# Splits for the second MoE tied to the first MoE's last block, and eight of its w_in blocks made float32 earlier

## The chip, the cores and the metric

The kernel runs on one core of a Trainium2 chip. The time is device microseconds (us) of one execution; "PE" is TensorE, "DVE" VectorE, "ACT" ScalarE, "POOL" GpSimd, "SP" the engine whose queue issues the DMAs.

## The reference

Causal attention with decay, then two mixture-of-experts layers (here plain two-layer blocks, called MoE 1 and MoE 2) over the same 2304 tokens. All inputs are float64 or float32 as NumPy draws them; the four weights are float64 here.

```python
attn = softmax(scale * q @ k.T + decay)       # 4 batches, 8 heads, 576 tokens, head size 64
x = (attn @ v) as 2304 x 512
h = x @ moe_w_in                               # 512 x 2048
x = (h * clip(h + 3, 0, 6) / 6) @ moe_w_out    # 2048 x 512
h = x @ moe2_w_in
out = softplus(h) @ moe2_w_out
```

## The kernel before

**Number format.** TensorE multiplies in a short format (fp32r), so every float32 operand is split into a high part (a copy by ACT in the short format) and a low part (original less high, by DVE or POOL), and each product is three matmuls.

**The order of the work.** Nothing is issued in the order of the program text. Every operation is registered with `op` or `dma` (lines 118 and 352) with the engines that may run it, an estimated cost, the keys that it reads (`r`) and writes (`w`), and a due time `at`. A planner, `Work.order` (line 152), then simulates the engines: at each step it takes the operation that can start first on its engine, and among those that can start equally early the one with the smallest `at`. Its result is the program order of each engine, fixed before the kernel runs. Engines work through their queues in order; a key read that another engine writes becomes a semaphore wait.

**MoE 1** works on five blocks of tokens: blocks 0 to 3 have 512, block 4 (`LAST_B`) 256. The 2048 inner columns are 16 units `ft` of 128. A unit of a block is 12 matmuls of the first product (`g1`, line 1299) into one PSUM bank, ACT's relu (line 1339), DVE's product (line 1341, its last reader of the bank, so the bank is free after it), the split of the result (copy, line 1319 or 1320; rest on DVE, line 1322), and 12 matmuls of the second product (`moe1_g2`, line 1362) that accumulate into four bank areas. The accumulators are evicted after unit 15 (lines 1390 and 1391); those of blocks 0 to 2 go through the two staging tiles `st`. Blocks 0, 1 and 2 run while attention of the next batch is computed in between. Blocks 3 and 4 run interleaved, unit by unit, and alone: their accumulators hold six of the eight banks, which leaves banks 2 and 3 for the first products. Relus of block 4 are the 256-wide ones in the trace.

**MoE 2** uses Strassen-like forms with seven products. Stage A (line 1415) works on 576 tokens by one pair `p` of units at a time, eight pairs; stage B (line 1516) follows. Before stage A can run, during blocks 3 and 4, these are prepared:

- `weights2_in(0, p, ...)`: the w_in of pair p, two blocks of 512 KB in float64. `raw_weights` (line 989) loads one and makes it float32 by bit operations: one on ACT (line 1017) and three on DVE (lines 1019, 1020, 1023). For p = 0, 2, 4, 6, 7 the tiles `st` stage it, for p = 1, 3, 5 the tile `HY`. Then four sums (line 1107) and three splits (lines 1136 on ACT, 1139 on DVE or POOL) make its seven operands in `rW`.
- `weights2_out(p, ...)`, p = 0 to 6: the w_out of pair p, float32 already in `wf_dram`; four sums (line 1107), seven splits (1136, 1139) into a ring in `XO`, seven stores to `wo_dram` (line 1166).
- `factors_x(0, ...)`: the first 576 tokens; four sums (line 1221) and seven splits (lines 1215, 1216).

**Conversions ahead of time.** `early2` (line 1068) loads one float64 block of MoE 2's weights to `st[0]` or `st[1]` in turn, makes it float32 and stores it to `wf_dram` (line 1073). The dictionary `early` (line 1566) says at which unit of which block: w_out blocks 0 to 7 at the even units of block 1, 8 to 15 at those of block 2. All others are in `late2` and are converted by `weights2`. Since `early2` of unit (t, 0) is registered ahead of the evictions of block t - 1 and uses the same `st`, these evictions come after it.

Of the kernel before, what the change touches and what calls it, by code (L numbers as in the profile page):

```python
# [273 lines left out]
def attention_two_moe_kernel(  # L274
# [22 lines left out]
    NF = moe_w_out.shape[0] // P  # L297
    TB = 512
    NB = (NT + TB - 1) // TB
    LAST_B = NB - 1  # L300
# [29 lines left out]
    op = wk.op  # L330
# [63 lines left out]
    three = mp.tile([P, 1], F32, name="three")  # L394
# [644 lines left out]
    def either(n, fn, late=K["pv"]):  # L1039

        return [("dve", dve(n), lambda: fn(nc.vector), late), ("pool", 2.8 * n + 60, lambda: fn(nc.gpsimd))]
# [30 lines left out]
        raw_weights(i, 1, o, ft, at, True)  # L1072
        dma(lambda: nc.sync.dma_start(out=wf_dram[o, ft], in_=words(i)[:, 0]), 4 * P * NC * P, r=[("stage", i), ("up", i)], w=[("wf", o, ft)], at=at - K["cvw"], name="storewf")

    def weights2(o, p, at, parts, i0):

        own = i0 >= 8

        def raw(i):
            return BIG["XO"][:, (i - 8) * NC * P:(i - 7) * NC * P].bitcast(F32)  # L1080

        for z in range(2):
            i, ft = i0 + z, 2 * p + z
            if not own and (o, ft) in late2:
                raw_weights(i, 1, o, ft, at, True)
                continue

            def load(i=i, ft=ft):
                dst = raw(i) if own else words(i)[:, 0]
                if wide:  # L1090
                    nc.sync.dma_start(out=dst, in_=wf_dram[o, ft])
                else:
                    nc.sync.dma_start(out=dst.rearrange("p (c f) -> p c f", c=NC) if o == 0 else dst, in_=w_source(1, o, ft))

            dma(load, 4 * P * NC * P, w=[("stage", i), ("up", i)] + [("o", i, 0), ("o", i, 1)] * (i < 2), r=["m2"] * (i in (2, 3) or own) + [("wf", o, ft)],
                at=at - 15, name="loadwf")
        h = 2 * P

        def x(i, e, j, n=1):
            if own:  # L1100
                return (BIG["XT"][:, i * 2 * h:] if e else raw(i0 + i))[:, j * h:(j + n) * h]
            return words(i0 + i)[:, e, j * h:(j + n) * h]


        def sums(dst, a, b, sub, r, w, name):
            def go(e):
                e.tensor_tensor(x(*dst), x(*a), x(*b), op=ALU.subtract if sub else ALU.add)
            op(either(h, go), r=r, w=w, at=at - 2, name=name)

        s0, s1, u0, u1 = ((x, 8 + i if own and x == "up" else i0 + i) for x in ("stage", "up") for i in range(2))  # L1110
        X11, X12, X21, X22 = (0, 0, 0), (0, 0, 1), (1, 0, 0), (1, 0, 1)
        Ca, Cb, Cc, Cd = (0, 1, 0), (0, 1, 1), (1, 1, 0), (1, 1, 1)
        if o == 0:
            sums(Ca, X21, X22, False, [s0, s1], [u0], "S1")
            sums(Cb, Ca, X11, True, [s0], [u0], "S2")
            sums(Cc, X11, X21, True, [s0, s1], [u1], "S3")
            sums(Cd, X12, Cb, True, [s0, u0], [u1], "S4")
        else:
            sums(Ca, X12, X11, True, [s0, s1], [u0], "T1")
            sums(Cb, X22, Ca, True, [s1], [u0], "T2")  # L1120
            sums(Cc, X22, X12, True, [s0, s1], [u1], "T3")
            sums(Cd, X21, Cb, True, [s1, u0], [u1], "T4")
        place = dict(zip(AT[o], ((0, 0, 0), (0, 0, 1), (0, 1, 0), (0, 1, 1), (1, 1, 0), (1, 1, 1), (1, 0, 1)) if o == 0 else
                         ((1, 0, 0), (1, 0, 1), (1, 1, 0), (1, 1, 1), (0, 1, 0), (0, 1, 1), (0, 0, 0))))
        for z0, z1, dst, w, then in parts:
            i, e, j = place[AT[o][z0]]
            n = z1 - z0

            def src(i=i, e=e, j=j, n=n):
                return words(i0 + i) if n == 4 else x(i, e, j, n)  # L1130

            def to(s, dst=dst, n=n):
                return dst(s).rearrange("p (e n) -> p e n", e=2) if n == 4 else dst(s)

            rd = [(s0, s1)[i], (u0, u1)[i]]
            op(("act", act(n * h, False), lambda src=src, to=to: nc.scalar.activation(out=to(0), in_=src(), func=ACTF.Copy)), r=rd, w=w, at=at, name="w2h")

            def lo(e, src=src, to=to):
                e.tensor_tensor(to(1), src(), to(0).bitcast(F32), op=ALU.subtract)  # L1139

            op(either(n * h, lo), r=rd, w=w, at=at, name="w2l")
            then()
# [15 lines left out]
    def weights2_out(p, at, i0):  # L1158

        parts = []  # L1160
        for z in range(7):
            i = pieces[0] % NPC
            pieces[0] += 1

            def store(z=z, i=i):
                dma(lambda: nc.sync.dma_start(out=wo_dram[p].rearrange("p (s z f) -> p s z f", s=2, z=7)[:, :, z], in_=piece(i).bitcast(F32)), 16 * P * P,
                    r=[("piece", i)], w=[("wo", p, z)], at=at, name="storewo")

            parts.append((z, z + 1, lambda s, i=i: piece(i)[:, s], [("piece", i)], store))
        weights2(1, p, at, parts, i0)  # L1170

    def load_wo(p, at):
        dma(lambda: nc.sync.dma_start(out=unit2_w(p).rearrange("p s z f -> p (s z f)").bitcast(F32), in_=wo_dram[p]), 4 * P * UW,
# [13 lines left out]
    def factors_x(t, at, step):  # L1187

        z = t % 2

        def pace(x):
            return [("pace", t - 1, x)] if t else []

        def sm(i):
            return BIG["XT"][:, i * n:(i + 1) * n].rearrange("p (c n) -> p c n", c=2)

        n = 2 * HA
        for f, c0, h in (("B11", 0, 0), ("B21", 2, 0), ("B22", 2, 1), ("B12", 0, 1)):
            a, done = t * NA + h * HA, 0
            while done < HA:  # L1200
                t1, o = divmod(a + done, TB)
                m = min(HA - done, tokens(t1) - o)

                def go(f=f, c0=c0, t1=t1, o=o, m=m, done=done):
                    to = sm(0) if f == "B12" else xf(z, f, 1).bitcast(F32)
                    nc.sync.dma_start(out=to[:, :, done:done + m], in_=x2_dram[t1][c0:c0 + 2, :, o:o + m].rearrange("c p s -> p c s"))

                dma(go, 8 * P * m, r=[("x2", t1, c) for c in (c0, c0 + 1)] + ["m2"], w=[("xt", 0) if f == "B12" else ("xf", z, f)], at=at, name="loadx2")
                done += m

        def raw(f):
            return xf(z, f, 1).bitcast(F32)

        def split(f, src, key, at, x):
            op(("act", act(n, False), lambda: nc.scalar.activation(out=xf(z, f, 0), in_=src(), func=ACTF.Copy)), r=[key] + pace(x), w=[("xf", z, f)], at=at, name="xfh")
            op(either(n, lambda e: e.tensor_tensor(xf(z, f, 1), src(), xf(z, f, 0).bitcast(F32), op=ALU.subtract)), r=[key], w=[("xf", z, f)], at=at, name="xfl")


        for i, (f, d, a, b) in enumerate((("T3", 1, "B22", 0), ("T1", 0, 0, "B11"), ("T2", 1, "B22", 0), ("T4", 1, "B21", 1))):
            def go(e, d=d, a=a, b=b):  # L1220
                e.tensor_tensor(sm(d), *((sm(y) if isinstance(y, int) else raw(y)) for y in (a, b)), op=ALU.subtract)  # L1221

            key = [("xt", y) if isinstance(y, int) else ("xf", z, y) for y in (a, b)]
            op(either(n, go), r=key + ["m2"] + pace(i), w=[("xt", d)], at=at + step * i, name="x" + f)
            split(f, lambda d=d: sm(d), ("xt", d), at + step * (i + 0.5), i)
        for i, f in enumerate(("B11", "B21", "B22")):
            split(f, lambda f=f: raw(f), "m2", at + step * (4 + i), 4 + i)
# [104 lines left out]
    def moe1_g1(t, ft):  # L1332
        at = moe_at(t, ft)
        n = tokens(t)
        bk = g1(0, t, ft, at, sorted({b for b, _ in acc_of(t)}) if ft == 0 else ())
        i, i3 = next_unit(t >= LAST_B - 1)
        g = gt[i][:, 0:n]
        ev = at - K["evb"]
        op(("act", act(n, True, 1), lambda: nc.scalar.activation(out=g, in_=bank[bk.i][:, 0:n], func=ACTF.Relu, bias=three)),  # L1339
           r=["three"], banks=[bk], w=[("g", i)], at=ev, name="relu")  # L1340
        op(("dve", dve(n), lambda: nc.vector.scalar_tensor_tensor(  # L1341
            out=g, in0=g, scalar=6.0, in1=bank[bk.i][:, 0:n], op0=ALU.min, op1=ALU.mult)),
           banks=[bk], w=[("g", i)], at=ev, name="g")
        split_g(g, i, i3, n, ev + K["splag"], 2)
        G[0, t, ft] = i3
# [217 lines left out]
        for o in range(2):  # L1563
            weights(o, ft, moe_at(0, ft) - K["cv"] + o * 2)

    early = {(1 + n // 8, n % 8 * 2): (1, n) for n in range(NF)} if wide else {}
    late2 = [(o, ft) for o in range(2) for ft in range(NF) if wide and (o, ft) not in early.values()]
    units = [(t, ft) for t in range(NB - 2) for ft in range(NF)]
    units += [(t, ft) for ft in range(NF) for t in (NB - 2, NB - 1)]
    for n in range(len(units) + 1):  # L1570
        if n < len(units):
            t, ft = units[n]
            if (t, ft) == (NB - 2, 0):
# [3 lines left out]
                at = moe_at(t, 0) - K["xl"]  # L1577
# [6 lines left out]
            if ft == NF - 1 and t + 1 < NB - 1:  # L1584

                at = moe_at(t + 1, 0) - K["xl"]
# [85 lines left out]
```

## Time and profile before

| | |
|---|---|
| timed runs | 1029.60, 1035.90, 1037.64 us; median 1035.9 |
| profiled execution | 1029.02 us |
| its span, first to last instruction | 1026.8 us |
| busy in the span | PE 95%, DVE 82%, ACT 58%, POOL 25% |

The 2.2 us between span and time lie outside the program. Times in the rows are us from the start of the span. Roughly: attention with blocks 0, 1 and 2 runs to 490, blocks 3 and 4 to 648, stage A to 836, stage B to the end. A line such as "PE ... [3.65 <-DVE GT L1341]" says that the engine sat idle for 3.65 us before it and what it waited for last.

### The profile page before, as it was taken

To read this page: it belongs to the slowest core of one execution; us is meant where nothing else is said; L and a number is where in the kernel's file an instruction comes from. 1 tells how busy PE (TensorE), PEld (TensorE's weight loads), DVE (VectorE), ACT (ScalarE), POOL (GpSimd) and SP (SyncE) were. 2 spreads that over 40 slices of the span, in tenths; PEclk is the share of its full clock that TensorE was granted. 3 is DMA by queue.
4 is the path that set the end of the run, shared out by engine and by line. 5 is a ranking of instruction groups with operands and counts; after the bars stand their busy time and mean duration, and the time that the engine had idled before them with its cause. 6 is when DMAs were issued, how large, how long until landed. Compare 5 with 4: busy or idle time off the path is not lost. (4 is left out here: it accounts for less than half of the span.)

```text
span 1026.8 us, 17687 instructions
## 1 busy us (share of the span) xinstructions
PE 979.6 (95%) x6116; PEld 849.7 (83%) x6116; DVE 843.0 (82%) x1671; ACT 596.5 (58%) x1300; POOL 255.7 (25%) x246
## 2 busy tenths in 40 slices
PE   8999998989999999999898899999999999999997
PEld 6666677768788888888787788899999999999997
DVE  8789879999998669986889886787787758888885
ACT  6899666778666556664454443665555544443342
POOL 2221332230000000000447532220010307454542
PEclk9999999999999999999999999999999999999999
DMA  6675553445553235412768550444333994445342
GB/s 139 165 156 144 132 154 100 110 143 148 141 146 93 61 115 144 117 47 68 238 210 264 165 173 11 162 145 146 131 122 143 346 368 138 124 135 152 108 126 77
DMA packets 189682, 149.12 MB, mean 145 GB/s; under 512 B 107948, under 2 KB 163660, under 8 KB 188696
## 3 DMA queue, kind: packets, MB, share of 16 engines
q1 hardware_dynamic: 189592, 147.99, 48.4%
q8 instruction: 48, 0.79, 0.3%
q14 instruction: 42, 0.34, 0.1%
HBM read 97.58 MB, written 50.37 MB: 144 GB/s over the span
## 5 line engine op out<-in xcount | busy, mean ns | idle before, releaser
L1299 PE MATMUL bank<-MX,W 128*128 128x512 f32 x768 | 224.5, 406 | 6.3 <-DVE GT L1341 5.6
L1362 PE MATMUL bank<-MX,W 128*128 128x512 f32 (+1 forms) x688 | 188.8, 383 | 3.6 <-DVE MX L1322 3.6
L1299 PEld LDWEIGHTS bank<-MX,W 128*128 128x128 f32 x768 | 133.9, 191 | 28.9 <-DVE GT L1341 6.1
L1362 PEld LDWEIGHTS bank<-MX,W 128*128 128x128 f32 x688 | 121.3, 189 | 25.9 <-DVE MX L1322 4.8
L1516 PE MATMUL bank<-rW,rW 128*128 128x256 f32 x1134 | 138.6, 283 | 1.9 <-POOL rW L1139 0.9
L1516 PEld LDWEIGHTS bank<-rW,rW 128*128 128x128 f32 x1134 | 136.8, 191 | 2.7 <-POOL rW L1139 1.1
L1415 PE MATMUL bank<-XO,rW 128*128 128x288 f32 x672 | 92.8, 298 | 3.6 <-DVE HY L1433 1.7
L1415 PEld LDWEIGHTS bank<-XO,rW 128*128 128x128 f32 x672 | 90.2, 188 | 5.7 <-DVE HY L1433 2.4
L710 ACT ACTIVATE p<-p,stats 64x64 f32<-64x64 f32 (+4 forms) x130 | 72.2, 556 | 33.6 <-DVE stats L701 32.5
L1495 ACT ACTIVATE rW<-st 128x512 fp32r<-128x512 f32 (+1 forms) x72 | 36.9, 518 | 76.9 <-PE bank L1516 42.9
L1036 POOL TENSOR_TENSOR W<-st,W 128x512 fp32r<-128x512 f32 x24 | 34.4, 1435 | 159.6 <-ACT W L1035 154.8
L1339 ACT ACTIVATE GT<-bank,three 128x512 f32<-128x512 f32 x80 | 51.1, 643 | 39.4 <-PE bank L1299 18.3
L1415 PE MATMUL bank<-MX,rW 128*128 128x288 f32 x480 | 70.2, 298 | 1.0 <-DVE HY L1433 1.0
L1415 PEld LDWEIGHTS bank<-MX,rW 128*128 128x128 f32 x480 | 65.7, 188 | 1.8 <-DVE HY L1433 1.4
L776 PE MATMUL bank<-ident,p 128*128 128x128 f32 x390 | 58.5, 276 | 8.6 <-DVE xs L861 4.4
L776 PEld LDWEIGHTS bank<-ident,p 128*128 128x128 f32 x390 | 46.2, 140 | 24.3 <-DVE xs L861 3.9
L581 POOL TENSOR_TENSOR V<-vr,V 128x640 fp32r<-128x640 f32 x10 | 16.7, 1670 | 189.9 <-ACT V L577 157.8
L811 ACT ACTIVATE pth<-bank 128x320 fp32r<-128x320 f32 (+2 forms) x100 | 42.5, 433 | 34.8 <-PE bank L776 26.0
L1499 POOL TENSOR_TENSOR rW<-st,rW 128x256 fp32r<-128x256 f32 (+1 forms) x35 | 40.1, 1150 | 80.7 <-ACT rW L1495 62.2
L1322 DVE TENSOR_TENSOR MX<-GT,MX 128x512 fp32r<-128x512 f32 (+1 forms) x69 | 52.2, 759 | 8.9 <-ACT MX L1319 8.2
L701 DVE CUSTOM_DVE_ANT_0 p<-bank,bar 64x64 f32<-64x64 f32 (+4 forms) x130 | 51.9, 420 | 8.0 <-PE bank L685 7.2
L1341 DVE SCALAR_TENSOR_TENSOR GT<-GT,bank 128x512 f32<-128x512 f32 x80 | 49.5, 626 | 8.4 <-ACT GT L1339 7.8
(219 smaller groups left out, 2103.8 us busy)
## 6 DMA issues: line engine op xcount, KB each, us to landing
st<-g_dram SPq DMA_DIRECT2D x36, 512.0 KB
st<-in_moe_w_out_dram SPq DMA_DIRECT2D x32, 512.0 KB
st<-in_moe_w_in_dram SPq DMA_DIRECT2D x26, 512.0 KB
wo_dram<-XO SPq DMA_DIRECT2D x49, 256.0 KB
g_dram<-HY SPq DMA_DIRECT2D x16, 576.0 KB
g_dram<-rBW SPq DMA_DIRECT2D x16, 576.0 KB
rW<-wo_dram SPq DMA_DIRECT2D x5, 1792.0 KB
qr<-in_q_dram SPq DMA_DIRECT2D x64, 72.0 KB
```

Of the source, the lines that this page charges most:

```text
L701: nc.vector.tensor_tensor_reduce(out=T["P"][par][ti][:r, a:c], in0=bank[bk.i][:r, o:o + c - a], in1=bar[:r, b0:b0 + c - a], op0=ALU.add, o ...
L710: nc.scalar.activation(out=pt, in_=pt, func=ACTF.Exp, scale=-1.0, bias=sv[:r, 0, ti:ti + 1], accum_out=sv[:r, 1, ti:ti + 1],)
L776: nc.tensor.transpose(acc[:, p0:p0 + P], T["P"][par][ti][:, k0:k0 + P], ident)
L811: nc.scalar.activation(out=place("PTH", j, ks, a, c), in_=src(), func=ACTF.Copy)
L1299: nc.tensor.matmul(bank[bk.i][:, 0:n], w[:, c], x[:, c, 0:n], start=(c == 0 and p == 0), stop=(c == NC - 1 and p == 2))
L1322: op(("dve", dve(n), lambda: nc.vector.tensor_tensor(t(glt), g, t(ght).bitcast(F32), op=ALU.subtract)), r=[("g", i), ("gh", i3)], w=[("gl" ...
L1339: op(("act", act(n, True, 1), lambda: nc.scalar.activation(out=g, in_=bank[bk.i][:, 0:n], func=ACTF.Relu, bias=three)), r=["three"], banks ...
L1341: op(("dve", dve(n), lambda: nc.vector.scalar_tensor_tensor(out=g, in0=g, scalar=6.0, in1=bank[bk.i][:, 0:n], op0=ALU.min, op1=ALU.mult)), ...
L1362: nc.tensor.matmul(bank[b][:, o:o + n], w[:, c * P:(c + 1) * P], x, start=(ft == 0 and p == 0 and o == 0), stop=(ft == NF - 1 and p == 2), ...
L1415: nc.tensor.matmul(bank[bks[b].i][:, 0:HA], wa[u][:, c], xa[v][:, c], start=(nm in ("P1", "P2", "P5") and c == 0 and y == 0), stop=(c == 1 ...
L1499: e.tensor_tensor(dst(1), src(), dst(0).bitcast(F32), op=ALU.subtract)
L1516: nc.tensor.matmul(bank[bks[b].i][:, o * 256:(o + 1) * 256], ga[u], wa[v], start=(p == 0 and o == 0 and y == 0), stop=(p == NPR - 1 and y ...
```

## The change

1. `weights2` gets a list of keys `pace` that its four sums and its splits read in addition. `weights2_out(p)` passes the key `("pace1", (3 * p + 1) // 2)`, and the relu of block 4, unit ft writes `("pace1", ft)`. So the work on pair p = 0 to 6 can't start before the relu of unit 0, 2, 3, 5, 6, 8, 9 of block 4. `weights2_in` passes none.
2. In `factors_x` for the first tokens (t = 0) the sums and splits read `("pace1", 11 + x * 2 // 3)`: the sums and splits of T3 and T1 wait for unit 11, of T2 for 12, of T4 for 13, the splits of B11, B21, B22 for units 13, 14, 15.
3. `early` gets eight entries more: w_in blocks 0 to 3 at units 9, 11, 13, 15 of block 1, and 4 to 7 at those units of block 2. They are no longer in `late2`, so pairs 0 to 3 load float32 from `wf_dram` during blocks 3 and 4.

```diff
-    def weights2(o, p, at, parts, i0):
+    def weights2(o, p, at, parts, i0, pace=()):
...
-            op(either(h, go), r=r, w=w, at=at - 2, name=name)
+            op(either(h, go), r=r + list(pace), w=w, at=at - 2, name=name)
...
-            rd = [(s0, s1)[i], (u0, u1)[i]]
+            rd = [(s0, s1)[i], (u0, u1)[i]] + list(pace)
...
-        weights2(1, p, at, parts, i0)
+        weights2(1, p, at, parts, i0, [("pace1", (3 * p + 1) // 2)])
...
         def pace(x):
-            return [("pace", t - 1, x)] if t else []
+            return [("pace", t - 1, x) if t else ("pace1", NF - 5 + x * 2 // 3)]
...
-           r=["three"], banks=[bk], w=[("g", i)], at=ev, name="relu")
+           r=["three"], banks=[bk], w=[("g", i)] + [("pace1", ft)] * (t == LAST_B), at=ev, name="relu")
...
-    early = {(1 + n // 8, n % 8 * 2): (1, n) for n in range(NF)} if wide else {}
+    early = {(1 + n // 8, n % 8 * 2): (1, n) for n in range(NF)} | {(1 + n // 4, n % 4 * 2 + 9): (0, n) for n in range(NF // 2)} if wide else {}
```

## Rows read from the trace of the kernel before

**Rows 1.** Windows: length, then busy us (instructions) PE, PEld, DVE, ACT, POOL; clock; DMA
```profile
320.00:380.00 60.00, 59.63 (x314) 49.04 (x313) 40.75 (x96) 31.16 (x74) 4.46 (x3) 1.00 0.28 74
...
450.00:490.00 40.00, 40.00 (x224) 33.38 (x223) 26.16 (x67) 21.27 (x53) 1.57 (x1) 1.00 0.21 63
500.00:570.00 70.00, 61.49 (x332) 51.69 (x331) 64.00 (x92) 32.16 (x76) 42.56 (x48) 0.98 0.66 216
570.00:620.00 50.00, 45.01 (x249) 37.66 (x248) 39.84 (x62) 24.43 (x48) 21.16 (x20) 1.00 0.56 177
620.00:640.00 20.00, 19.96 (x117) 17.44 (x116) 12.24 (x20) 6.77 (x13) 4.81 (x5) 1.00 0.00 1
640.00:680.00 40.00, 36.75 (x249) 34.14 (x249) 30.77 (x52) 24.59 (x48) 9.49 (x8) 1.00 0.47 154
```

**Rows 2.** Waits of PE from 495 to 645: us in total, times, longest
```profile
PE bank L1299 <- DVE GT L1341: 12.1, 8, 3.6
```

**Rows 3.** Timeline of ACT: relus of block 4 (0, 12, 15), factors_x's last split, stage A's first eviction
```profile
501.85 0.47 ACT L1339 ACTIVATE GT<-bank,three 128x256 f32<-128x256 f32 x1 [0.52 <-PE bank L1299]
...
619.18 0.47 ACT L1339 ACTIVATE GT<-bank,three 128x256 f32<-128x256 f32 x1 [1.54 <-DVE MX L1322]
...
621.25 0.69 ACT L1215 ACTIVATE XO<-XO 128x576 fp32r<-128x576 f32 x1
...
641.94 0.46 ACT L1339 ACTIVATE GT<-bank,three 128x256 f32<-128x256 f32 x1
...
650.55 0.41 ACT L1430 ACTIVATE HY<-bank 128x288 f32<-128x288 f32 x1
```

**Rows 4.** Chain of waits: groups of three matmuls back to back, 256 and 512 wide
```profile
544.89 0.35 PE bank L1362 x3
545.25 0.69 PE bank L1299 x3
```

**Rows 5.** Timeline of PE: two waits
```profile
507.56 1.65 PE L1299 MATMUL bank<-MX,W 128*128 128x512 f32 x3 [3.65 <-DVE GT L1341]
...
565.89 0.97 PE L1299 MATMUL bank<-MX,W 128*128 128x512 f32 x3 [1.93 <-DVE GT L1341]
```

**Rows 6.** Timeline of DVE: its queue during these two waits, and one split later
```profile
502.21 0.96 DVE L1019 TENSOR_SCALAR HY<-HY 128x512 uint32<-128x512 uint32 x1
503.10 0.95 DVE L1139 TENSOR_TENSOR XO<-XT,XO 128x256 fp32r<-128x256 f32 x1
503.97 0.94 DVE L1019 TENSOR_SCALAR HY<-HY 128x512 uint32<-128x512 uint32 x1
504.83 2.34 DVE L1020 SCALAR_TENSOR_TENSOR HY<-HY 128x512 uint32<-128x512 uint32 x2
...
563.42 1.22 DVE L1023 SCALAR_TENSOR_TENSOR HY<-HY 128x512 uint32<-128x512 uint32 x1
...
569.80 0.41 DVE L1139 TENSOR_TENSOR XO<-XT,XO 128x256 fp32r<-128x256 f32 x1
```

**Rows 7.** Groups by line and shape: busy us, mean ns of one | idle before
```profile
L1023 DVE SCALAR_TENSOR_TENSOR st<-st 128x512 uint32<-128x512 uint32 x58 | 46.1, 797 | 0.6
L1020 DVE SCALAR_TENSOR_TENSOR st<-st 128x512 uint32<-128x512 uint32 x58 | 45.2, 782 | 4.1 <-ACT st L1017 2.6
L1019 DVE TENSOR_SCALAR st<-st 128x512 uint32<-128x512 uint32 x58 | 25.8, 448 | 8.8 <-DMA st<-in_moe_w_in_dram 7.7 <-DMA wo_dram<-XO 0.8
```

**Rows 8.** Timeline of SP: early conversions' stores, first and last of nine, last of all
```profile
234.94 0.32 SPq L1073 DMA_DIRECT2D wf_dram<-st  x1
...
320.06 0.35 SPq L1073 DMA_DIRECT2D wf_dram<-st  x1
...
441.98 0.34 SPq L1073 DMA_DIRECT2D wf_dram<-st  x1
```

**Rows 9.** Timeline of DVE: first evictions of blocks 1 and 2 through `st`
```profile
374.35 0.69 DVE L1391 TENSOR_SCALAR st<-bank 128x512 f32<-128x512 f32 x1 [0.20 <-PE bank L1362]
...
497.28 1.39 DVE L1391 TENSOR_SCALAR st<-bank 128x512 f32<-128x512 f32 x2
```

## The prediction

> **What bounds the kernel now.** I read the windows first, to find where TensorE is not busy, then PE's waits there, then the queues of the engine waited for, and last the windows of the stretches that receive the moved work. From 320 to 380 and from 450 to 490 PE is busy 59.63 of 60 and 40.00 of 40 us [rows 1]: PE is the bound there, and VectorE has 19.2 and 13.8 us to spare. From 500 to 620 PE is idle for 8.51 + 4.99 = 13.5 us, and from 640 to 680 for another 3.25 [rows 1]. In the first of these the wait is nearly always one: the first product of a unit waits for line 1341, eight times and 12.1 us in all [rows 2]. That line is the last reader of a first-product bank; with two such banks left while blocks 3 and 4 run, PE stops as soon as VectorE is late with it. VectorE is busy 64.0 of 70 us from 500 to 570 [rows 1], so line 1341 stands in a queue of conversions and splits.
>
> How much is lost there? Three matmuls take 0.35 us at 256 columns and 0.69 to 0.70 at 512 [rows 4]; a unit of blocks 3 and 4 has 24 of each width, so 8 x 0.35 + 8 x 0.70 = 8.4 us. The relus of units 0 and 12 of block 4 are 619.18 - 501.85 = 117.3 us apart [rows 3] where 12 x 8.4 = 100.8 would do: 16.5 us are lost, 13.5 of them visible as idle time. A part of the rest is the clock: 0.98 over 70 us [rows 1] is 1.4 us of work at full speed, lost at the lower of the two levels (1.2 instead of 2.4 GHz), and the longest wait, 3.65 us [rows 5], lies in that window.
>
> **The change, part by part.** *Conversions taken out of blocks 3 and 4.* A conversion costs VectorE 0.448 + 0.782 + 0.797 = 2.03 us by the group means [rows 7]; eight of them take at least 16.2 us out of VectorE's 64.0, which leaves 47.8 of 70, or 68%. ACT loses eight operations as well, but at 32.16 of 70 us it is not the bound [rows 1]. Two waits are plainly theirs. At 502.21 VectorE begins conversions in HY of 0.96 + 0.94 + 2.34 us around one split of 0.95, and PE starts again only at 507.56 after 3.65 us [rows 5, 6]. At 563.42 another (1.22 us) stands in the queue while PE waits 1.93 us [rows 5, 6]. With the 1.4 us of clock behind the first that is 3.65 + 1.4 + 1.93 = 7.0 us; I count all of it as gain. If the split ahead of line 1341 were enough to keep the first wait, 0.95 of it would stay: the lower end is 6.0. What is late next is the splits themselves.
>
> *Less load and pacing against the other waits.* 16.5 - 7.0 = 9.5 us remain. They come from splits ahead of line 1341 and from the burst of factors_x just before 621.25 [rows 3]. Ends: 0 (any split still gets in the way) and 9.5 (none does). From 620 to 640, where VectorE is busy 12.24 of 20 us (61%), PE is busy 19.96 [rows 1]; the stretch to 570 comes down to 68%, near that row, but from 570 to 620 the conversions of the later pairs stay and VectorE's 39.84 of 50 falls only by what pacing moves behind unit 12. I take half, 4.7 us.
>
> A paced split on ACT waits for nothing new, because the relu runs on ACT itself. On VectorE a paced sum waits for the relu, and behind it stands line 1341 of that unit, which waits for the same relu. So the added waits cost nothing where the planner puts them in that order; a sum put much ahead would hold the queue, and this stays inside the range.
>
> *Conversions put into blocks 1 and 2.* Eight more, so 8 x 2.03 = 16.2 us of VectorE, 8.1 in each block, plus eight loads of 512 KB and eight stores of 256 KB on SP's queue, and 256 KB reloaded where 512 KB was loaded before. They can't run sooner than the two staging tiles come free: nine stores take from 234.94 to 320.06, or 10.6 us per conversion [rows 8]. So the four of block 1 fall behind 320, where VectorE has 19.2 us to spare, and those of block 2 behind 441.98, where it has 13.8 [rows 1, 8]. DMA is busy 0.28 and 0.21 there. Cost between 0 and 16.2 (all of it on the path); I take 1, near the lower end, because PE runs full beside a VectorE of this load in both rows.
>
> *The handover to stage A.* The splits of factors_x, all issued by 621.25 [rows 3], move in steps to the relu of unit 15, 641.94 on the old clock. ACT's part of such a split takes 0.69 us, stage A's first eviction is at 650.55 [rows 3], and B22, the last paced operand, is used by the last of the seven products. I count 0; ends are -3.25 (the idle time of 640 to 680 goes) and +4 (half the 8.6 us from 641.94 to 650.55 is added).
>
> **Sum.** -7.0 - 4.7 + 1 + 0 = -10.7 us. From the profiled execution, 1029.02 (span 1026.8 and 2.2 outside), that is 1018.3; from the median 1035.9 it is 1025.2. Of four executions two lie at 1029 and two at 1036 to 1038, so I take the middle of their spread, 1032.7, and forecast 1022. About 1% is what a measurement here can tell from no change, 10.4 us.
>
> **Rivals.**
> 1. *Full recovery.* All 16.5 us and some of the 3.25 go, nothing is given back: about -17, 1016. For it speaks the 620 to 640 window; against it that the later pairs still convert from 570 to 620.
> 2. *Only the conversions count.* Pacing puts the same splits elsewhere, and line 1341 stands behind them as before: -7.0 + 1 = -6, 1027. For it: a 256-wide split on VectorE takes 0.95 us at 503.10 and 0.41 at 569.80 [rows 6], so splits released together may stretch each other. The Trainium skill ("SBUF — State Buffer", section "Who interferes with whom") gives a reason: a VectorE instruction with two SBUF inputs and a GpSimd instruction that reads SBUF exclude each other through a shared port. By that rule pacing, which frees four sums and seven splits for both engines at one relu, keeps the long form; the trace's 0.95 against 0.41 agrees.
> 3. *Late at the handover.* The paced splits of factors_x collide with the evictions after unit 15, PE starts stage A late by the 4 us above, and the other splits keep two thirds of the remaining waits: -7.0 - 3.2 + 1 + 4, about -5, 1028; with rival 2's waits as well about -2, 1031.
> 4. *Slower: the staging tiles are late at the block ends.* The evictions of block 1 use the same tiles and come after the thirteenth conversion (twelve of block 1 and the one of unit (2, 0)). At 10.6 us each the last is stored at 320.06 + 4 x 10.6 = 362.5, 11.9 us ahead of 374.35 [rows 8, 9]; in block 2 at 441.98 + 42.4 = 484.4, 12.9 us ahead of 497.28. It decides from (374.35 - 320.06)/4 = 13.6 us per conversion. At 17.5 us each both evictions are late by 15 us, the accumulators stay taken, and if PE covers a third with first products 2 x 10 are added: -10.7 + 20 = +9, 1042. For it: these conversions rank behind attention in due time. Against: behind 320 VectorE is idle a third of the time [rows 1], and DMA mostly.
>
> **How the numbers follow.** Forecast 0.47, rival 1 0.15, rival 2 0.16, rival 3 0.12, rival 4 0.10. The forecast's gains lie from 7 to 14 us, 1018 to 1026; something over two thirds of it is beyond 10.4, 0.34, and with rival 1 and a little of rival 2 by the spread of runs faster is 0.51. Slower takes most of rival 4, 0.09. The rest, 0.40, is within 1%. The range for 8 in 10 reaches from 1010 (full recovery from the lower cluster would be 1012) to 1036 (rival 3 with the spread of runs); it leaves out rival 4 and the far ends.
>
> **What would show it.** Right: no line 1019 on HY before 570, the units of block 4 about 8.7 us apart from 0 to 12, the wait of PE on line 1341 down from 12.1 us to 4 or less, the early stores ending near 363 and 484, evictions of blocks 1 and 2 released by PE as before, and PE still full from 320 to 490. Wrong: waits on line 1341 that keep their sum with splits in VectorE's queue instead of conversions (rival 2), PE idle at the block ends with an eviction waiting for a DMA (rival 4), stage A's first products waiting for lines 1215 or 1216 (rival 3), or a sum that waits for a relu with line 1341 of an earlier unit behind it.

## The result and the profile after

The changed kernel took 1021.04 us in the median of four runs (1019.44 to 1022.26), beside 1033.69 us for the kernel before (four runs, the three of the table above among them): ratio 0.9895, 95% interval 0.9863 to 0.9927. (This ratio is not the quotient of the two medians, which is 0.9878; experiments are compared by the ratio.) The profiled execution took 1020.33 us, its span is 1018.3 us, 8.5 us shorter than before.

Windows of the kernel after, in the columns and stretches of [rows 1]:

```profile
320.00:380.00 60.00, 58.89 (x309) 48.81 (x308) 47.80 (x103) 33.50 (x78) 4.93 (x3) 1.00 0.41 114
450.00:490.00 40.00, 40.00 (x226) 33.34 (x225) 32.04 (x78) 21.95 (x54) 1.57 (x1) 1.00 0.33 105
500.00:570.00 70.00, 67.99 (x377) 58.52 (x376) 49.20 (x77) 29.61 (x70) 37.46 (x42) 0.98 0.56 181
570.00:620.00 50.00, 45.96 (x256) 38.90 (x256) 42.01 (x60) 23.16 (x48) 26.59 (x30) 1.00 0.62 198
620.00:640.00 20.00, 19.00 (x113) 16.53 (x112) 15.59 (x22) 10.26 (x20) 7.14 (x5) 1.00 0.12 34
640.00:680.00 40.00, 38.10 (x273) 36.68 (x272) 32.62 (x55) 26.47 (x54) 8.28 (x9) 1.00 0.54 178
```

Read the first two against the third. In blocks 1 and 2 VectorE now works 7.1 and 5.9 us more and PE stays at 58.9 of 60 and 40.0 of 40. From 500 to 570 VectorE falls from 64.0 to 49.2 us, and PE's idle time from 8.51 to 2.01 us; the granted clock is 0.98 as before, so the 1.4 us lost there to the lower level (1.2 in place of 2.4 GHz) were lost again. From 570 to 620 VectorE has more to do than before (42.0 against 39.8), and PE still stands idle for 4.0 of 50 us. From 620 to 640 PE, which had been full, loses 1.0 us.

Waits of PE from 495 to 645 us (total, times, longest), after, against [rows 2]:

```profile
PE bank L1299 <- DVE GT L1341: 4.8, 5, 1.8
PE bank L1362 <- DVE MX L1322: 1.2, 1, 1.2
PE bank L1362 <- DVE SB L1322: 1.0, 1, 1.0
```

The wait on line 1341 is down from 12.1 to 4.8 us; second products wait 2.2 us for line 1322, 1.3 us (in two waits) before. What stands in VectorE's queue while PE waits for the longest of these is seen in the timelines. VectorE first, then the relu on ACT whose result this line 1341 reads, then PE:

```profile
535.74 0.96 DVE L1139 TENSOR_TENSOR XO<-XO 128x256 fp32r<-128x256 f32 x1
536.62 1.22 DVE L1322 TENSOR_TENSOR MX<-GT,MX 128x512 fp32r<-128x512 f32 x1
537.76 0.95 DVE L1139 TENSOR_TENSOR XO<-XT,XO 128x256 fp32r<-128x256 f32 x1
538.64 0.94 DVE L1107 TENSOR_TENSOR st<-st,st 128x256 f32<-128x256 f32 x1
539.50 0.67 DVE L1341 SCALAR_TENSOR_TENSOR GT<-GT,bank 128x512 f32<-128x512 f32 x1
```

```profile
537.93 0.69 ACT L1339 ACTIVATE GT<-bank,three 128x512 f32<-128x512 f32 x1 [2.30 <-DVE MX L1322]
```

```profile
540.23 1.20 PE L1299 MATMUL bank<-MX,W 128*128 128x512 f32 x3 [1.78 <-DVE GT L1341]
```

No conversion is left here, as there was in [rows 6]; a sum and two splits of 256 columns, all in the long form of 0.94 to 0.96 us, stand in the queue. Only the sum runs wholly between the end of the relu, 538.62, and line 1341. The relu itself is late by the same queue: it began at 537.93, after ACT had been idle for 2.30 us, because it waited for line 1322 (1.22 us), which stood behind the first of the two splits. Elsewhere conversions of the later pairs are still in the way: the timeline of VectorE shows them ahead of line 1341 in two more of the five waits, 1.27 us to 574.51 and 0.88 us to 598.44.

Timeline of ACT after: the relus of units 0, 12 and 15 of block 4, the last split of factors_x and stage A's first eviction, as in [rows 3]:

```profile
503.42 0.47 ACT L1339 ACTIVATE GT<-bank,three 128x256 f32<-128x256 f32 x1 [2.62 <-PE bank L1299]
...
611.08 0.48 ACT L1339 ACTIVATE GT<-bank,three 128x256 f32<-128x256 f32 x1 [0.49 <-DVE MX L1322]
...
635.75 0.45 ACT L1339 ACTIVATE GT<-bank,three 128x256 f32<-128x256 f32 x1
636.10 0.68 ACT L1215 ACTIVATE XO<-XO 128x576 fp32r<-128x576 f32 x1
...
644.09 0.43 ACT L1430 ACTIVATE HY<-bank 128x288 f32<-128x288 f32 x1
```

Units 0 to 12 now take 611.08 - 503.42 = 107.7 us, 9.0 each, instead of 117.3; at full speed it would be 100.8. The last split of factors_x starts 0.35 us after the relu of unit 15, as the new key says, and stage A starts without a wait. PE's first matmuls of stage A, after:

```profile
642.97 8.29 PE L1415 MATMUL bank<-XO,rW 128*128 128x288 f32 x59
```

The early stores of SP after (ninth, last of block 1, last two of block 2), against [rows 8]:

```profile
320.55 0.35 SPq L1073 DMA_DIRECT2D wf_dram<-st  x1
...
355.39 0.32 SPq L1073 DMA_DIRECT2D wf_dram<-st  x1
...
468.82 7.31 SPq L1073 DMA_DIRECT2D wf_dram<-st  x2
```

Four more conversions take 34.8 us from the ninth store on, 8.7 us each. The first evictions through `st` come well after the stores, for block 1 on ACT, for block 2 on VectorE [rows 9]:

```profile
378.88 0.60 ACT L1390 ACTIVATE st<-bank 128x512 f32<-128x512 f32 x1 [0.37 <-PE bank L1362]
```

```profile
498.79 1.39 DVE L1391 TENSOR_SCALAR st<-bank 128x512 f32<-128x512 f32 x2
```

To place gains and losses I cut each span at three marks of its timeline: the relu (line 1339) of unit 0 of block 1, that of block 3, and stage A's first matmul (line 1415). For the kernel before these are 245.0, 495.9 and 649.55 us.

| us | blocks 1, 2 | blocks 3, 4 | both | stages A, B |
|---|---|---|---|---|
| before | 250.9 | 153.7 | 404.5 | 377.3 |
| after | 250.7 | 145.6 | 396.3 | 375.3 |

Blocks 3 and 4 give 8.1 us, stages A and B 2.0, blocks 1 and 2 cost nothing. The run after comes to the first mark 1.7 us later, which no part of the change explains. These are lengths of one profiled execution each.

### The profile page after: what moved, and what is told of

Read it like the earlier page. It is cut to its first block, busy times and chain, and to the rows that moved or that the text cites. A ratio compares the mean times of both kernels' runs of the same rounds, so it can differ in the third digit from the quotient of the medians.

```text
span 1018.3 us, 17717 instructions
## 1 busy us (share of the span) xinstructions
PE 978.4 (96%) x6116; PEld 850.4 (84%) x6116; DVE 838.2 (82%) x1662; ACT 599.8 (59%) x1309; POOL 256.4 (25%) x245
## 4 chain that ended last, share of the span: by engine, by line
PE 67%; DVE 19%; issue 5%; ACT 3%; DMA 3%; POOL 2%; SPq 1%; DVEq 0%; POOLq 0%; ACTq 0%
PE bank L1516 16%; PE bank L1415 15%; PE bank L1299 13%; PE bank L1362 13%; PE bank L685 4%; PE bank L846 3%; PE bank L776 3%; DVE MX L1322 2%; DVE st L1020 2%; DVE GT L1341 1%; DVE st L1023 1%; DVE p L701 1%; DMA st<-in_moe_w_in_dram 1%; DVE KB L632 1%; DVE QA L632 1%
```

## Experiments

The question after the result was which part brings what. The theory on record is two terms: conversions leave VectorE's queue (7.0 us), and pacing with less load thins the splits in it (4.7 us). Against it stand: one part does it all; the early conversions aren't free where they went; and, after the long forms in the queue above, that it is not the number of operations but their length while GpSimd works too that makes line 1341 late. Each timed run is compared with the kernel before on its chip; the stage lengths come from each run's one profile, with the marks above.

**1. One part alone.** The first kernel has the new `early` and no pacing, the second both pacings and the old `early`.

```diff
 (kernel before, early conversions only)
-    early = {(1 + n // 8, n % 8 * 2): (1, n) for n in range(NF)} if wide else {}
+    early = {(1 + n // 8, n % 8 * 2): (1, n) for n in range(NF)} | {(1 + n // 4, n % 4 * 2 + 9): (0, n) for n in range(NF // 2)} if wide else {}
 (kernel after, pacing only)
-    early = {...} | {(1 + n // 4, n % 4 * 2 + 9): (0, n) for n in range(NF // 2)} if wide else {}
+    early = {...} if wide else {}
```

> The eight early conversions alone, no pacing. My theory (conversions worth 7.0 us less 1 given back, pacing worth 4.7 on its own): ratio 0.994, about 6 us under the kernel before. Rival, only the conversions count: nearly the whole gain of the change, 0.990. Rival, pacing is what counts: 0.998 or more, with PE's waits on line 1341 still above 9 us from block 3 on.

> Both pacings alone, pairs 0 to 3 convert in blocks 3 and 4 as before. My theory: 4.7 us under the kernel before, 0.9955, and the waits in which a conversion in HY stands ahead of line 1341 are still there. Rival, only the conversions count: 1.000. Rival, pacing is what counts: 0.991.

The early conversions alone: 1024.15 us, ratio 0.9937 (0.9916 to 0.9958). Pacing alone: 1026.88 us, 0.9957 (0.9940 to 0.9975). In microseconds of 1031 that is 6.5 and 4.4, together 10.9; both parts together gave 10.8, and 9.1 when measured once more (experiment 2). So each part has its own share: both intervals lie below 1, and pacing alone is clear of the whole change. The early conversions alone aren't: their interval overlaps with those of the change, and only the stage lengths below set them apart. But the place is not where I had put it. Waits of PE with the early conversions alone:

```profile
PE bank L1299 <- DVE GT L1341: 9.4, 8, 2.1
PE bank L1362 <- DVE MX L1322: 2.1, 2, 1.3
```

and with pacing alone:

```profile
PE bank L1299 <- DVE GT L1341: 8.0, 10, 2.0
```

With the conversions gone the wait of 3.65 us is gone too (the longest is 2.1), but the sum on line 1341 falls by 2.7 us only. By VectorE's timeline mostly splits and sums take the conversions' place in its queue, as ahead of the longest wait, which ends at 505.65; ahead of the wait that ends at 597.60 (2.03 us) are conversions of the later pairs. Blocks 3 and 4 take 149.9 us with the first kernel (-3.7) and 148.6 with the second (-5.1); stages A and B 374.8 and 375.9. Of the 3.7 us only 2.0 are idle time of PE; the rest is its busy time, and the clock accounts for most of that: from 500 to 570 it is 1.00 in this profile, 0.98 before.

**2. Which pacing?** The change without the pacing of factors_x, and the change without that of w_out:

```diff
 (without pacing of factors_x)
-            return [("pace", t - 1, x) if t else ("pace1", NF - 5 + x * 2 // 3)]
+            return [("pace", t - 1, x)] if t else []
 (without pacing of w_out)
-        weights2(1, p, at, parts, i0, [("pace1", (3 * p + 1) // 2)])
+        weights2(1, p, at, parts, i0)
```

> The change without the pacing of factors_x. If the w_out pacing carries the pacing's share, the ratio stays at that of the change, 0.990, and factors_x again comes in a burst before unit 12. If factors_x's pacing carries it, 0.994. If pacing factors_x costs time at the handover (as rival 3 has it), 0.988.

> The change without the pacing of the w_out splits. If the w_out pacing carries the pacing's share: 0.994, with waits on line 1341 from the first units on behind splits of pairs 0 and 1. If factors_x's pacing carries it: 0.990. If neither does (only the conversions count): 0.990 here and in the run without factors_x's pacing alike, and in the one with the early conversions alone.

> The changed kernel once more, beside the others on one chip. The runs so far give 0.990 with an interval of 0.6%, and 0.993 without either of the two pacings. If both pacings are needed together it stays at 0.990; if either does the work of both it comes out at 0.992 to 0.993.

1023.70 us, 0.9932 (0.9907 to 0.9957), and 1023.26 us, 0.9929 (0.9905 to 0.9953); the changed kernel once more, on another chip with its own runs of the kernel before, 1021.45 us, 0.9912 (0.9894 to 0.9931). By the ratios each pacing is worth about 2 us beside the other, but the intervals overlap, and the profiles don't rank them: blocks 1 to 4 take 397.3 us without the pacing of factors_x, 393.9 without that of w_out and 395.5 with both, stages A and B 376.0, 377.7 and 375.6. Which pacing does more stays open.

**3. Are the early conversions free?** This kernel doesn't make the eight early conversions at all, and the first pairs load float32 blocks that are there already:

```diff
-    early = {...} | {(1 + n // 4, n % 4 * 2 + 9): (0, n) for n in range(NF // 2)} if wide else {}
-    late2 = [(o, ft) ... if wide and (o, ft) not in early.values()]
+    early = {...} if wide else {}
+    late2 = [(o, ft) ... if wide and (o, ft) not in early.values() and not (o == 0 and ft < 8)]
...
-                    nc.sync.dma_start(out=dst, in_=wf_dram[o, ft])
+                    nc.sync.dma_start(out=dst, in_=wf_dram[1, ft])
```

> The changed kernel with the eight early conversions left out and nothing in their place: pairs 0 to 3 load float32 blocks of w_out where their w_in belongs, so the conversion of eight w_in blocks is left out. It prices what blocks 1 and 2 pay. My theory: nothing, since the way from block 1's first relu to block 3's first took 250.9 us before and 250.7 with the change; so 0.991 as the changed kernel, and 250 to 251 us on that way. Rival, the 16 us of VectorE are partly on the path: 0.987 or less and 246 to 248 us.

1019.30 us, 0.9878 (0.9854 to 0.9903). Blocks 1 and 2 take 249.8 us without the eight conversions, 250.7 and 249.8 in the two profiles with them. The timed difference to the changed kernel, 0.9878 against 0.9895 and 0.9912, is 2 to 3.5 us with overlapping intervals: the price of the eight is not told apart from nothing. Where the profiles differ is not in blocks 1 and 2 either but in blocks 3 and 4, 143.6 us here against 145.6 and 145.7, and there the clock differs: from 500 to 560 it loses 1.7 us in both profiles of the change and nothing here (last section). Two rows show the cover, the windows from the first mark to the second (columns as in [rows 1]). Before:

```profile
245.00:495.90 250.90, 247.47 (x1335) 204.45 (x1334) 204.75 (x487) 154.13 (x357) 12.72 (x8) 1.00 0.39 111
```

After:

```profile
246.70:497.40 250.70, 246.79 (x1335) 204.64 (x1335) 215.06 (x504) 161.58 (x371) 13.21 (x8) 1.00 0.47 136
```

VectorE does 10.3 us more and ACT 7.5 in a stretch as long as before, and PE has the same 1335 matmuls. 46 us of VectorE were idle there.

**4. More of them, and sooner.** Sixteen, twelve and ten early conversions instead of eight, and the eight at units 1, 3, 5 and 7 instead of 9 to 15. The new part of `early` reads:

```python
{(1 + n // 8, n % 8 * 2 + 1): (0, n) for n in range(NF)}                          # 16
{(1 + n // 6, n % 6 * 2 + 5): (0, n) for n in range(12)}                          # 12
{(1, n * 2 + 9) if n < 4 else (2, n * 2 - 3): (0, n) for n in range(10)}          # 10, four in block 1
{(1 + n // 4, n % 4 * 2 + 1): (0, n) for n in range(NF // 2)}                     # 8, sooner
```

> All sixteen w_in blocks early, at the odd units of blocks 1 and 2; no conversion is left in blocks 3 and 4 and in the handover. Rival 4's mechanism: seventeen conversions before the evictions of block 1 and the two staging tiles at 9 to 10.6 us each end at 388 to 415, 10 to 40 us behind the 377 at which block 1 ends, so the evictions wait and the ratio is 0.995 to 1.01. If the tiles turn round faster than that (VectorE and DMA are idle there), nothing waits, the remaining waits from 560 to 610 go too, and the ratio is 0.985.

> Twelve w_in blocks early, six each in blocks 1 and 2: fifteen conversions before the evictions of block 1, ending at 370 to 390 by 9 to 10.6 us each, at the edge. If the tiles are in time: two pairs fewer convert in blocks 3 and 4, 2 to 3 us under the changed kernel, 0.987. If they are late: 0.990 or more, with PE waiting where block 2 begins.

> Ten w_in blocks early, four in block 1 and six in block 2, so pair 4 too loads float32. Twelve cost 3 us between the first relus of blocks 1 and 3 (after taking off the matmuls that only changed places) and took about as much out of blocks 3 and 4. If the price comes from block 1, which is fuller, ten with two more in block 2 are nearly free: 1 to 2 us under the changed kernel, 0.989 to 0.990. If any conversion more than eight is on the path: 0.991 to 0.993.

> The eight early conversions at units 1, 3, 5, 7 of blocks 1 and 2 instead of 9, 11, 13, 15. If the two staging tiles set the pace, the order of the conversions changes and not their times: the last store of block 1 again near 355, and 0.991. If the due unit decides, conversions crowd into the first halves, where VectorE is busy 94%, and it costs 2 to 4 us: 0.993 to 0.995.

| early conversions | median us | ratio (95%) | blocks 1, 2 | blocks 3, 4 | both |
|---|---|---|---|---|---|
| 8 (the change, again) | 1021.45 | 0.9912 (0.9894 to 0.9931) | 249.8 | 145.7 | 395.5 |
| 10 | 1024.19 | 0.9923 (0.9900 to 0.9946) | 254.1 | 143.1 | 397.2 |
| 12 | 1021.37 | 0.9928 (0.9905 to 0.9952) | 256.5 | 140.4 | 396.8 |
| 16 | 1023.67 | 0.9932 (0.9915 to 0.9949) | 259.5 | 140.4 | 399.9 |
| 8, sooner | 1023.14 | 0.9924 (0.9900 to 0.9946) | 253.3 | 143.7 | 397.1 |

None is shown to be faster than the change, and by the intervals none is shown to be slower. With 16 neither expectation came true: no eviction waited for a tile, and nothing was gained. With 12 and 16 the blocks 3 and 4 gain 5 us more, and blocks 1 and 2 give them back and a little more. (Part of that is order alone: with 10, 12 and 16 conversions, 9, 12 and 14 second products of 512 columns, 2 to 3 us, lie ahead of the second mark instead of behind it. So the column "both" is the one to read.) For 16, from mark to mark:

```profile
246.20:505.70 259.50, 253.53 (x1349) 206.39 (x1347) 224.88 (x525) 170.95 (x386) 12.74 (x8) 1.00 0.51 151
```

PE is idle for 5.97 us here, 3.91 in the change. Idle time alone doesn't explain the longer stretch, though: over blocks 1 to 4 PE idles 10.2 us with 16 conversions and 11.0 in the change, and what grows is its busy time for the same matmuls, 389.8 against 385.3 us. Some 1.7 us of that are the clock, which lost 3.4 us in blocks 3 and 4 of this run and 1.7 in the change; where the rest comes from isn't shown. The staging tiles are not what gives out. With 16 the last stores of block 1, on SP, stand at

```profile
364.88 0.90 SPq L1073 DMA_DIRECT2D wf_dram<-st  x2
```

and the first eviction through `st` at 377; with the eight sooner the last one is at 343.14, 12 us sooner than in the change, and no gain is seen.

**5. What do the other eight conversions still cost?** This kernel makes no conversion in blocks 3 and 4; pairs 4 to 7 load w_out's float32 blocks in place of w_in's:

```diff
-            if not own and (o, ft) in late2:
+            s = 1 if (o, ft) in late2 else o
+            if False:
...
-                    nc.sync.dma_start(out=dst, in_=wf_dram[o, ft])
+                    nc.sync.dma_start(out=dst, in_=wf_dram[s, ft])
```

> The changed kernel with no conversion in blocks 3 and 4 at all: pairs 4 to 7 load float32 blocks of w_out where their w_in belongs, so the conversion of eight w_in blocks is left out. It shows what the remaining conversions cost. By the price of the first four pairs (3.7 us of the stage where they were taken out alone) 3 to 4 us under the changed kernel, 0.986 to 0.987. If what is left of PE's waits is due to the splits, under 1 us, 0.990.

1014.56 us, 0.9855 (0.9835 to 0.9875), 4 to 6 us below the changed kernel by the ratios; blocks 3 and 4 take 137.4 us. Its windows, where the changed kernel still had 2.0 and 4.0 us of idle PE:

```profile
500.00:570.00 70.00, 68.00 (x385) 58.67 (x385) 50.96 (x80) 30.06 (x71) 39.14 (x45) 1.00 0.58 191
570.00:620.00 50.00, 50.00 (x289) 43.69 (x288) 33.52 (x56) 23.29 (x47) 20.50 (x23) 1.00 0.50 157
```

Without the later conversions PE is full from 570 to 620, with VectorE at 33.5 of 50 us instead of 42.0. So these eight are a good part of what remained; more, by the ratios, than the 3 to 4 us expected. The stretch to 570 keeps its 2.0 us. Blocks 3 and 4 are 8.2 us shorter than in the change: 5.1 are idle time of PE, of which 4.0 lie between 570 and 620 and 1.0 behind 620, and the rest is its busy time, 1.4 of it by the clock (0.98 over the first 70 us in the change, 1.00 here). This profiled execution was the fastest of its five, 1010.03 us, so the profile shows more than the median does.

**6. Is it the length beside GpSimd?** The changed kernel with `weights2`'s sums and splits on VectorE alone. VectorE gets more operations, not fewer:

```diff
-            op(either(h, go), r=r + list(pace), w=w, at=at - 2, name=name)
+            op(either(h, go)[:1], r=r + list(pace), w=w, at=at - 2, name=name)
...
-            op(either(n * h, lo), r=rd, w=w, at=at, name="w2l")
+            op(either(n * h, lo)[:1], r=rd, w=w, at=at, name="w2l")
```

> The changed kernel with the sums and splits of MoE 2's weights on VectorE alone, none on GpSimd. From the first relu of block 3 on VectorE spends 29.3 + 10.9 = 40.2 us on its 50 of them between 490 and 610, and GpSimd 59.9 us on its 67. If the long form of the 256-wide ones on VectorE (0.95 against 0.41 us) is GpSimd's presence, as the Trainium skill's page 'SBUF — State Buffer' has it, all of them take the short form: some 100 of 256 columns at 0.41 and the wider ones are about 52 us instead of 40.2, the conversions and line 1322 get shorter as well, and the time is within 3 us of the changed kernel, 0.988 to 0.994. If the long form has another cause, VectorE gets GpSimd's share at 0.7 each, 47 us more, and the ratio is above 1.01.

1013.47 us (1011.59 to 1015.83), ratio 0.9825 (0.9802 to 0.9847). This is the lowest median of all; its interval lies below both of the changed kernel's. The expectation, at most 3 us of gain, was too small. Its windows:

```profile
500.00:570.00 70.00, 70.00 (x398) 60.81 (x397) 52.30 (x122) 34.26 (x81) 2.13 (x3) 1.00 0.56 182
570.00:620.00 50.00, 50.00 (x287) 43.43 (x286) 40.49 (x90) 23.38 (x48) 0.00 (x0) 1.00 0.61 196
```

PE is busy for the whole 120 us. VectorE runs 212 instructions there instead of the change's 137, in 92.8 us instead of 91.2. And its waits of PE from 495 to 645:

```profile
PE bank L1362 <- DVE SB L1322: 0.5, 1, 0.5
```

Line 1341 makes PE wait no more. Nor is the relu held up much by line 1322 (ACT's waits in the same stretch, after and with VectorE alone):

```profile
ACT GT L1339 <- DVE MX L1322: 12.2, 10, 2.6
```

```profile
ACT GT L1339 <- DVE MX L1322: 3.0, 5, 0.9
```

The groups of splits of `w_out` from 500 to 620 (busy us, mean ns) show what became shorter. After:

```profile
L1139 DVE TENSOR_TENSOR XO<-XT,XO 128x256 fp32r<-128x256 f32 x13 | 9.1, 707 | 0.0
L1139 DVE TENSOR_TENSOR XO<-XO 128x256 fp32r<-128x256 f32 x9 | 8.4, 938 | 0.2 <-ACT XO L1136 0.2
```

On GpSimd, after:

```profile
L1139 POOL TENSOR_TENSOR XO<-XT,XO 128x256 fp32r<-128x256 f32 x15 | 14.2, 949 | 8.3 <-ACT XO L1136 8.3
L1139 POOL TENSOR_TENSOR XO<-XO 128x256 fp32r<-128x256 f32 x12 | 12.0, 1016 | 0.3 <-ACT XO L1136 0.3
```

With VectorE alone:

```profile
L1139 DVE TENSOR_TENSOR XO<-XT,XO 128x256 fp32r<-128x256 f32 x28 | 11.2, 418 | 0.0
L1139 DVE TENSOR_TENSOR XO<-XO 128x256 fp32r<-128x256 f32 x21 | 8.0, 418 | 0.0
```

49 splits on VectorE alone take 19.2 us; 22 of them beside GpSimd took 17.5. The 27 that GpSimd took over saved VectorE 1.7 us, and left it with single operations up to twice as long in the queue of lines 1322 and 1341. Blocks 3 and 4 take 135.9 us here; 16 units of 8.4 us are 134.4. Stages A and B take 378.3, 3.0 more than in the change; why isn't shown. The planner also makes another order for this kernel, and no run takes the share of the order from that of the shorter operations. The rule weighed in rival 2 is borne out: the Trainium skill ("SBUF — State Buffer", section "Who interferes with whom") says that a VectorE instruction with two SBUF inputs and a GpSimd instruction that reads SBUF hold each other up at a shared port. The trace agrees: taking GpSimd's part away brings 418 ns on average for these splits.

## Why the prediction was right, and where not

The forecast was 1022.0 us in a range of 1010 to 1036; measured were 1021.0 and, the second time, 1021.5. On the profiled execution's own scale the sum was -10.7 and the profile gives 1020.33 - 1029.02 = -8.7. That the total came so near is in part luck: blocks 3 and 4 gave 8.1 us where the two terms have 11.7, and the conversions that cost nothing in blocks 1 and 2 and 2.0 us in stages A and B, which no part of the change is shown to cause, made up for most of it; a start 1.7 us later took some back.

- *Conversions taken out, -7.0.* Alone and timed, with their price in blocks 1 and 2, they gave 6.5 us where the sum has 7.0 - 1 = 6. In its place the term was too large: blocks 3 and 4 gave 3.7 us in the profile of that kernel, not 7. The step that failed is "I count all of it as gain". The 3.65 us wait went, but PE's waits on line 1341 still came to 9.4 us, and those on line 1322 went from 1.3 to 2.1: with a conversion out of the queue a split or a sum stood there, as the lower end had it for one of the waits and as it proved to be for most. Of 5.58 us of waits PE's idle time gave back 2.0. The 1.4 us of clock came back in that kernel (1.00 from 500 to 570), but not in the change, where the clock fell behind another wait (0.98 again). The prediction also read only what stood ahead of line 1341; it left out that the relu before it waits for line 1322 in the same queue (12.2 us in all after, experiment 6). The other 2.5 us that this kernel's profile is shorter lie in stages A and B.
- *Less load and pacing, -4.7.* Pacing alone was timed at 4.4 us, and blocks 3 and 4 shrank by 5.1 us in its profile. Size right. No paced operation of VectorE is seen to wait for a relu between 495 and 645, as the argument had it. The share of "less load" can't be taken apart from the first term: there the two terms of blocks 3 and 4 are 3.7 + 5.1 = 8.8 where the change gave 8.1, and the forecast 11.7.
- *Conversions put into blocks 1 and 2, +1.* By the ratios they cost 2 to 3.5 us, not told apart from nothing, and -0.2 in the profile. The cover named (VectorE's idle time behind 320 and 442) held for eight; with 10 or more the stretch grew.
- *Handover, 0.* Stage A began with no wait and no splits in its way. What moved there is seen just ahead: from unit 12 to stage A's first matmul it is 642.97 - 611.08 = 31.9 us, 30.4 before, in the window where PE had been full. That is the 1.5 us between the 9.6 us gained by unit 12 and the 8.1 of the table. That the paced splits of factors_x take it isn't shown: without their pacing the same way takes 33.3 us.
- *Stages A and B, not in the sum.* They came out 2.0 us shorter; the end of -3.25 had allowed for it. But the kernels with the new `early` lie between 373.6 and 378.3, and pacing alone gave 375.9, so that no part of the change is shown to be its cause.

Of the rivals, the first (16.5 us back) is the size of experiment 6's gain (18 us of 1031), which took GpSimd out of the splits, not of the change's. The second was half right: splits in the long form did take the conversions' place, but pacing alone counted for 4.4 us all the same. The third fell at 642.97, where stage A begins without a wait. The fourth fell at the stores: 8.7 us per conversion in place of 10.6, far from the 13.6 at which it decides, and with sixteen early conversions the stores still were 11 us ahead of the eviction. "What would show it" held for the unit spacing (9.0, said 8.7) and the stores (355 and 476, said 363 and 484); the waits on line 1341 stopped at 4.8 where 4 was the mark, and line 1019 has no work between 490 and 560 (nor up to 570), as the windows of that line after show (DVE busy and count, clock, DMA share, GB/s). The eight counted ahead of it lie in blocks 1 and 2:

```profile
320.00:380.00 60.00, 1.68 (x4) 1.00 0.41 114
450.00:490.00 40.00, 1.70 (x4) 1.00 0.33 105
490.00:560.00 70.00, 0.00 (x0) 0.98 0.59 192
```

## What to carry to other kernels

When an engine's queue makes another wait, read every operation ahead of the awaited one with its duration before pricing the removal of one kind: what moves up into its place may cost nearly the same. Ask as well what holds up the operation that the awaited one reads: it may wait in the same queue. Operations that don't matter soon can be tied to the progress of the engine that they disturb, and work can be moved under a stretch where the bound engine is full; here eight conversions went there at no price that could be told from nothing, and ten or more gave no gain, though VectorE still had idle time. And a helper engine that stretches the operations of the busy one can be worth less than nothing: compare the duration of the same operation with the helper at work and idle.

## What the runs showed of the hardware

**Work taken over from GpSimd cost VectorE almost nothing.** I had the two durations, 0.95 and 0.41 us [rows 6], ahead of the prediction and used them only against pacing. The runs price them: the change with GpSimd left out of the splits gained another 0.7 to 0.9% (0.9895 or 0.9912 to 0.9825). Operations of other lines get shorter as well, such as the splits of line 1322 from 500 to 620. After, and with VectorE alone:

```profile
L1322 DVE TENSOR_TENSOR MX<-GT,MX 128x512 fp32r<-128x512 f32 x9 | 7.9, 876 | 0.1
```

```profile
L1322 DVE TENSOR_TENSOR MX<-GT,MX 128x512 fp32r<-128x512 f32 x10 | 6.9, 688 | 0.5 <-ACT MX L1319 0.2
```

**The same program doesn't start the same.** Up to the relu of unit 0 of block 0 no edit changes anything, yet this relu falls between 91 and 96 us. The windows from 9 to 21 us show where. Before:

```profile
9.00:21.00 12.00, 11.39 (x53) 7.29 (x53) 10.59 (x35) 8.70 (x27) 0.00 (x0) 1.00 0.75 171
```

and with the pacing of factors_x left out:

```profile
9.00:21.00 12.00, 11.58 (x32) 7.32 (x33) 7.14 (x27) 5.67 (x18) 0.00 (x0) 0.57 0.75 172
```

The granted clock is 1.00 in one and 0.57 in the other, most of that stretch at the lower level (1.2 GHz in place of 2.4), and PE got through 32 matmuls in place of 53 with the same busy time. No edit reaches this place. Over the fourteen profiles the clock of this window is 1.00 in five, 0.86 in five, 0.72 in two and 0.57 in two, and the relu comes at 91.0 to 92.2, 92.3 to 92.8, 94.3 to 94.5 and 95.5 to 96.0 us: the lower the clock, the later. It is a part of the spread between runs, and a reason to compare stages rather than spans.

**A wait of the same length lowered the clock in one run and not in another.** Windows after the wait of 1.78 us in the kernel after:

```profile
536.00:540.00 4.00, 2.44 (x18) 2.11 (x17) 4.00 (x5) 0.69 (x1) 3.84 (x5) 1.00 1.02 340
540.00:545.00 5.00, 4.77 (x15) 3.90 (x16) 0.17 (x1) 0.00 (x0) 0.86 (x2) 0.66 0.16 52
```

and with the eight conversions left out, where PE is idle for 1.78 us too:

```profile
540.00:545.00 5.00, 3.22 (x20) 2.71 (x19) 3.78 (x5) 0.69 (x1) 4.31 (x6) 1.00 0.96 323
545.00:550.00 5.00, 5.00 (x28) 4.23 (x27) 1.35 (x3) 1.52 (x3) 0.00 (x0) 1.00 0.00 0
```

The first lost 0.34 x 5 = 1.7 us of work to the clock behind its wait, as much as the wait itself; the second lost nothing. What decides between them isn't shown. The second profile of the change lost about as much at this wait as the first. So a stage length carries the clock too: in blocks 3 and 4 it fell somewhere in six of the fourteen profiles, at a price of 1.7 us in five of them and 3.4 in the one with sixteen conversions.
